# Moving every tile that the matrix engine reads onto a 128-byte line

## The chip, the cores and the metric

The kernel runs on one core of one Trainium2 chip. The metric is device time in microseconds (us). The kernel before took 677.31 us, the median of three runs (676.64 to 678.71).

## What is computed

The reference is windowed attention with sinks, followed by a two-layer feed-forward block. In short:

```python
scores = q @ k.T / sqrt(64)                 # 4 batches, 8 heads, 768 positions, head_dim 64
keep   = (key < 4) | ((0 <= row - key) & (row - key < 128))
a      = softmax(where(keep, scores, -1e9))
x      = (a @ v)                            # heads side by side: 3072 tokens x 512
h      = x @ w_in                           # 512 -> 2048
g      = max(h, 0) + alpha * min(h, 0)
out    = g @ w_out                          # 2048 -> 512
```

The weights arrive as 64-bit floats and the kernel turns each into a high and a low 32-bit part.

## The kernel before, in words

The 3072 tokens are handled as 12 chunks of 256 rows (`QC`), numbered `c`. The hidden dimension of 2048 is cut into 16 slices of 128, numbered `f`. A chunk has two parts of work. Its attention makes the rows `x`, held as a high part `xh` and a low part `xl`, each four blocks of 128 x 256. Then the feed-forward block runs over the 16 slices.

One step (c, f) of the feed-forward block has two groups of matmuls on the matrix engine (PE). The first group, `gemm1` on line L894, is 12 matmuls of 128x128 against 128x256: the stationary operand (loaded into the array ahead of the matmul) is a block of the weight tile `w`, and the moving operand (streamed through) is `xh` or `xl`. The scalar engine (ACT) and the vector engine (DVE) then make `g` (L898, L899) and split it into `gh` and `gl` (L900, L901). The second group, `gemm2`, is 6 matmuls of 128x128 against 128x512 (L931, L932, L929; the very last step has them on L916 to L918): here `gh` or `gl` is stationary and the weight tile `w` moves. `gemm2` of a step runs two steps (`LAG`) behind `gemm1`, so PE has other work while ACT and DVE make `g`.

Attention of the next chunk is spread over the steps of the current one. From chunk 2 on, a head's `q` and `k` are copied from the loaded tile `stage` into a tile `kq` (L561 to L565): `k` with a high part in 64 partitions and a low part in the other 64, and `q` as `qh` and `ql`. The scores are two matmuls per half head, L597 with `qh` stationary and L598 with `ql` stationary, and the moving operand is `k`, mostly 260 columns wide. In the tile before, `k` comes first (392 columns), then `qh`, then `ql`. The matmuls with the values are on L786 and L875. Heads alternate between two `kq` tiles. Chunks 0 and 1 read `stage` directly (L588).

A planner in the kernel (`Plan`) fixes the order of all instructions from estimated costs. Which of several buffers an operation gets also comes from it. It knows nothing of addresses. In the first microseconds PE runs fill matmuls (L1086) on a small tile `idle`, whose one column is read over and over, 512 columns wide.

Where a tile lies in SBUF follows from the order in which tiles are asked for and from their sizes, rounded up to 32 bytes. Each partition has the same layout, so one address stands for a tile. With the sizes in the code, the tiles that PE reads begin at these bytes past a multiple of 128 (from the addresses in the two built programs):

| tile | read by PE as | before | with the change |
|---|---|---|---|
| `xh`, `xl` | moving, gemm1 | 96 | 0 |
| `w` of slices 0 to 13 and 15 | stationary gemm1, moving gemm2 | 32 | 0 |
| `w` of slice 14 | the same | 64 | 0 |
| `gh`, `gl` | stationary, gemm2 | 96 | 0 |
| `k` in the two `kq` tiles, first half of the rows | moving, scores | 96 and 0 | 0 and 0 |
| the same, second half (132 columns on) | moving, scores | 112 and 16 | 16 and 16 |
| `qh`, `ql` in the two `kq` tiles | stationary, scores | 0 and 32 | 0 and 0 |
| `v` | stationary, values | 32 | 0 |
| `ident` | moving, transposes | 64 | 0 |
| `sinkT`, `vs` | sinks | 96 | 0 |
| `comb`, `wa` | moving, values | 0 | 0 |
| `stage`, `pt_` (read by PE in chunks 0 and 1 alone) | scores, transposes | 32, 64; 32, 64, 96 | 0, 32; 64, 96, 0 |

All blocks that a matmul takes out of these tiles begin a whole multiple of 128 bytes into the tile, except the second half of `k`.

Of the kernel before, what the change touches and what calls it, by code (L numbers as in the profile page):

```python
# [9 lines left out]
F32 = mybir.dt.float32  # L10
F32R = mybir.dt.float32r
# [4 lines left out]
I32 = mybir.dt.int32  # L16
# [3 lines left out]
P = 128  # L20
B, H, S, D = 4, 8, 768, 64
DM, DF = 512, 2048
NS = 4
WIN = 2 * P + NS
QC = 2 * P
KC = 3 * P + 2 * NS
CPB = S // QC
NCHUNK = B * CPB
NF = DF // P
# [49 lines left out]
class Plan:  # L79
# [20 lines left out]
    def held(self, tile_):  # L100
        v = Value(None)
        v.at = tile_
        return v

    def op(self, engine, cost, run, reads=(), writes=(), tail=0.09, mode=None, nbytes=0, other=None, locks=False):
        o = Op(engine, cost, tail, run, self.rank if engine == "PE" else None)
        o.ways = {engine: (cost, run)}
        if other:
            o.ways[other[0]] = other[1:]
        o.born = self.rank  # L110
        if engine == "PE":
            self.rank += 1
        o.mode, o.nbytes, o.index = mode, nbytes, len(self.ops)
        seen = []
        for group, writing in ((reads, False), (writes, True)):
            for x in group:
                v, key = x if isinstance(x, tuple) else (x, None)
                if v not in seen:
                    seen.append(v)
                keys = [k for k in set(v.wrote) | set(v.read) if key is None or k is None or k == key]  # L120
                for k in keys:
                    o.before.update(v.wrote.get(k, ()))
                    if writing:
                        o.before.update(v.read.get(k, ()))
                if writing:
                    for k in keys:
                        if key is None or k == key:
                            v.wrote.pop(k, None)
                            v.read.pop(k, None)
                    v.wrote.setdefault(key, []).append(o)  # L130
                else:
                    v.read.setdefault(key, []).append(o)
        for v in seen:
            v.left += 1
        o.values = seen
        o.takes = [v for v in seen if v.kind]
        o.locks = locks
        self.ops.append(o)
        return o
# [144 lines left out]
def dve(n, fast=False):  # L284
    return 0.07 + (0.52e-3 if fast else 1.04e-3) * n


def cast(n, psum=False):
    return (0.045 if psum else 0.092) + 0.84e-3 * n
# [32 lines left out]
def program(ctx, tc, qk, pairs, vp, vq, vs, w, par, out):  # L322
    nc = tc.nc
    const = ctx.enter_context(tc.tile_pool(name="const", bufs=1))
# [10 lines left out]
    def several(name, n, shape, dtype):  # L335
        plan.kind(name, [pool.tile(shape, dtype, name=f"{name}{i}") for i in range(n)])
# [2 lines left out]
    plan.kind("swap", [scratch.tile([4, P, P], F32, name=f"swap{i}") for i in range(2)])  # L339
    plan.kind("turns", [scratch.tile([4, P, 2 * 32], F32, name=f"turns{i}") for i in range(2)])  # L340
    trid = held(scratch.tile([P, 2, P], F32, name="trid"))
    several("stage", 2, [P, QC + KC], F32)
    several("kq", 2, [P, KC + 2 * QC], F32R)
    several("v", 4, [P, 3, 2, D], F32)
    several("pt_", 3, [P, 2, WIN], F32)
    several("comb", 5, [P, 4 * P], F32)
    several("wa", 2, [P, 2 * DM], I32)
    several("sink", 2, [P, 2, H, NS], F32)
    several("nm", 2, [P, H, 2], F32)
    several("sm", 2, [P, H, 2], F32)  # L350
    several("ri", 4, [P, 8], F32)
    several("jk", 3, [P, 2], F32)
    several("ts", 1, [P, 2, 4, 32], F32R)
    several("sinkT", 1, [P, QC], F32R)
    several("vs", 1, [P, DM], F32R)
    several("ob", 2, [P, DM], F32)
    several("xh", 2, [P, KT, QC], F32R)
    several("xl", 2, [P, KT, QC], F32R)
    several("g", 2, [P, QC], F32)
    several("gh", LAG + 1, [P, QC], F32R)  # L360
    several("gl", LAG + 1, [P, QC], F32R)

    size = const.tile([P, NF], F32, name="size")
    sizes = held(size)
    raws, fins = {}, {}

# [41 lines left out]
    stage, vtile, vst = {}, {}, {}  # L408
# [3 lines left out]
    def lend(f, shape, count):  # L412
        box = {}

        def part(i):
            if "tile" not in box:
                box["tile"] = const.tile([P, count, *shape], F32, tag=f"w{f}", name="lent")
            return box["tile"][:, i]
        out_ = []
        for i in range(count):  # L420
            v = held(None)
            v.bind, v.box = lambda i=i: part(i), box
            out_.append(v)
        lent[f] = out_
        return out_

    early = lend(NF - 1, [QC + KC], 3) + lend(NF - 2, [QC + KC], 1)
    shared = const.tile([P, 1, QC + KC + 4 * WIN], F32, tag=f"w{NF - 2}", name="lent")
    early[3].box["tile"] = shared[:, :, :QC + KC]
    early_v = lend(NF - 3, [3, 2, D], 4)  # L430

    def bound(v):
        if v.at is None:
            v.at = v.bind()
        return v.at

    def load_head(c, h):
# [4 lines left out]
        src = pairs[c, h // 2] if c in SPLIT else qk[c, h]  # L442
        op("SP", ISSUE, lambda: nc.sync.dma_start(bound(t), src), writes=[t], nbytes=4 * P * (QC + KC))

# [71 lines left out]
    masks = pool.tile([P, 3, WIN], BF16, name="masks")  # L516
    ident = const.tile([P, P], F32, name="ident")
    tri = pool.tile([P, 2, P], F32, name="tri")
    fm = const.tile([P, 2 * H], F32, name="fm")
    flag = const.tile([1, 1], I32, name="flag")  # L520

    setup("POOL", 0.2, lambda: nc.gpsimd.iota(rel[:, 0:P], pattern=[[-1, P]], base=P, channel_multiplier=1), (), ("rel",))
# [24 lines left out]
    xh, xl, prep, comb, sink, ptile_, sums, rinv, nms, wt = {}, {}, {}, {}, {}, {}, {}, {}, {}, {}  # L547
# [4 lines left out]
    def prep_head(c, h):  # L552
        st = stage.pop((c, h))
        if c in SPLIT:
            r = slice(h % 2 * D, (h % 2 + 1) * D)
            prep[c, h] = (st, r)
            return
        kq = val("kq")
        ks, qh, ql = [lambda s=s: kq.at[:, s] for s in (slice(0, KC), slice(KC, KC + QC), slice(KC + QC, KC + 2 * QC))]
        q_raw, k_raw = lambda: st.at[:, :QC], lambda: st.at[:, QC:]  # L560
        op("ACT", cast(KC), lambda: nc.scalar.copy(ks(), k_raw()), reads=[st], writes=[(kq, "k")])  # L561
        op("ACT", cast(QC), lambda: nc.scalar.copy(qh(), q_raw()), reads=[st], writes=[(kq, "q")])
        op("DVE", dve(KC), lambda: nc.vector.tensor_tensor(ks()[D:], k_raw()[D:], ks()[D:].bitcast(F32), ALU.subtract),  # L563
           reads=[st], writes=[(kq, "k")])
        op("DVE", dve(QC), lambda: nc.vector.tensor_tensor(ql(), q_raw(), qh().bitcast(F32), ALU.subtract),  # L565
           reads=[st, (kq, "q")], writes=[(kq, "l")])
        prep[c, h] = (kq, qh, ql, ks)

    def unit(c, h, u):
# [6 lines left out]
        qs = slice(u * P, (u + 1) * P)  # L576
        w0 = slice(0 if c % CPB or u else P, WIN)
        n = w0.stop - w0.start
# [24 lines left out]
    def soften(c, h, u, s):  # L603
        if u == 0:
            ptile_[c, h] = val("pt_")
        pt, nm, sm = ptile_[c, h], nms[c], sums[c]
        i = min((c % CPB) * 2 + u, 2)
        w0 = slice(0 if i else P, WIN)
# [9 lines left out]
    def finish_head(c, h):  # L618
# [5 lines left out]
        if c in SPLIT:  # L624
            op("POOL", 0.17, lambda: nc.gpsimd.tensor_copy(sk.at[:, :, h], pt.at[:, :, P:P + NS]), reads=[pt], writes=[(sk, h)])
            tp = bank(c, h, "pa")
            for u in range(2):
                o = 2 * u * P
                both = u > 0 or c % CPB > 0

# [5 lines left out]
            t = val("comb")  # L636
            o = P if c % CPB == 0 else 0
            op("ACT", cast(4 * P - o, True), lambda: nc.scalar.copy(t.at[:, o:], tp.at[:, o:]), reads=[tp], writes=[t],
# [10 lines left out]
        for u in range(2):  # L649
            if u == 0 and c % CPB == 0:  # L650
                op("DVE", 0.2, lambda: nc.vector.tensor_scalar(view()[:, 0], pt.at[:, 0, P + NS:], ri.at[:, 0:1], None, op0=ALU.mult),
# [13 lines left out]
    sinkT = {}  # L665
# [282 lines left out]
    def attention(c):  # L948
        def a_step(h, u):
            def run():  # L950
                if u == 0:
                    if h == 0 and c == PAIRED:
                        masks_in_order()
                    if h == 0 and c and c % CPB == 0:
                        vs_prep(c // CPB)
                    prep_head(c, h)
                    next_load()
                unit(c, h, u)
                if u == 1:
                    finish_head(c, h)  # L960
                    first = 1 if c >= PAIRED else 5
                    if h in range(first, first + (KT if c >= PAIRED else 2)):
                        load_v(c, h - first)
            return run
# [139 lines left out]
    with tc.If(bad != 0):  # L1104
# [3 lines left out]
        with tc.For_i(0, B, 1) as b:  # L1108
            for cc in range(CPB):
# [4 lines left out]
                for j in range(2):  # L1114
                    ob = gen.tile([P, DM], F32, tag="ob", name="ob", bufs=3)
# [162 lines left out]
```

## Time and profile before

| | |
|---|---|
| runs | 678.71, 677.31, 676.64 us, median 677.31 |
| profiled execution, first to last instruction | 676.2 us; its own device time is not shown, the span is 1.1 us under the median |
| busy share of the span | PE 98%, PE weight loads 86%, DVE 78%, ACT 59% |
| mean granted PE clock | 0.994 |
| gemm1 matmuls | 2304 |
| gemm2 matmuls on L931, L932, L929 | 382 each |

A PE row's busy time overlaps its neighbours', because a matmul starts before the one ahead of it has left the array. So the length of a matmul says little about its cost. What counts is the time from one start to the next, which is called spacing below. It is read from a timeline, where each row has a start to a hundredth of a microsecond; over a run of n matmuls the spacing is the distance of two starts divided by n.

### The profile page before, as it was taken

The numbers are of one execution on the slowest core, as the hardware profiler recorded it, in microseconds if no ns is written. First come the engines' busy times: TensorE is split into PE (matmuls) and PEld (weight loads), VectorE is DVE, ScalarE is ACT, GpSimd is POOL, SyncE is SP. The second block draws the span as 40 slices with busy tenths as digits, with TensorE's granted clock in tenths as the row PEclk, the third lists the DMA queues.
The fourth block names the chain that finished last, engine by engine and source line by source line (L and its number), as shares of the span: only waits on it lengthen the run. The fifth ranks groups of instructions, "written<-read, shape, count | busy, mean of one in ns | idle before, by whom it ended". The sixth has DMA issues, their size and how long they took to land.

```text
span 676.2 us, 13243 instructions
## 1 busy us (share of the span) xinstructions
PE 663.8 (98%) x4532; PEld 580.5 (86%) x4534; DVE 525.8 (78%) x1750; ACT 397.5 (59%) x1066; POOL 34.5 (5%) x115
## 2 busy tenths in 40 slices
PE   9989999999999999999999999999999999999996
PEld 4577898888989989989988988988998988998995
DVE  6999999968967976986986995995895994994331
ACT  6989888827636726736636735644744753853332
POOL 2110000001000000000000000010000000000000
PEclk9979999999999999999999999999999999999999
DMA  8684641424343453443443433552542543420001
GB/s 314 229 277 151 241 187 39 127 71 147 122 133 107 122 148 93 145 132 95 141 118 114 143 107 93 163 140 61 172 128 78 161 128 88 142 94 17 32 2 35
DMA packets 58683, 85.19 MB, mean 126 GB/s; under 512 B 9072, under 2 KB 35056, under 8 KB 58608
## 3 DMA queue, kind: packets, MB, share of 16 engines
q1 hardware_dynamic: 55056, 71.17, 34.7%
q10 hardware_dynamic: 3552, 13.11, 5.4%
q8 instruction: 37, 0.61, 0.4%
q14 instruction: 38, 0.31, 0.1%
HBM read 67.22 MB, written 17.04 MB: 125 GB/s over the span
## 4 chain that ended last, share of the span: by engine, by line
PE 83%; DVE 9%; ACT 5%; issue 2%; POOL 0%; DMA 0%; ACTq 0%; SPq 0%; POOLq 0%
PE bank L894 35%; PE bank L931 12%; PE bank L932 11%; PE bank L929 11%; PE bank L786 3%; PE bank L598 3%; PE bank L597 3%; PE bank L875 2%; DVE wa L396 2%; ACT pt L614 1%; ACT wa L382 1%; DVE wa L394 1%; DVE w L404 1%; DVE g L899 1%; DVE gl L901 1%
## 5 line engine op out<-in xcount | busy, mean ns | idle before, releaser
L894 PE MATMUL bank<-xh,w 128*128 128x256 f32 x1536 | 307.9, 283 | 0.4 <-DVE g L899 0.2
L894 PEld LDWEIGHTS bank<-xh,w 128*128 128x128 f32 x1536 | 250.6, 189 | 9.0 <-DVE g L899 3.0
L894 PE MATMUL bank<-xl,w 128*128 128x256 f32 x768 | 215.1, 280 | 0.1
L898 ACT ACTIVATE g<-bank,param 128x256 f32<-128x256 f32 x192 | 90.5, 472 | 117.4 <-PE bank L894 113.1
L931 PE MATMUL bank<-w,gh 128*128 128x512 f32 x382 | 151.7, 397 | 0.2 <-ACT gh L900 0.2
L932 PE MATMUL bank<-w,gh 128*128 128x512 f32 x382 | 150.1, 393 | 0.0
L894 PEld LDWEIGHTS bank<-xl,w 128*128 128x128 f32 x768 | 145.2, 189 | 4.4 <-DVE xl L808 0.3
L614 ACT ACTIVATE pt<-pt,nm 128x260 f32<-128x260 f32 (+1 forms) x192 | 94.5, 493 | 53.5 <-DVE nm L610 53.1
L899 DVE TENSOR_TENSOR g<-bank,g 128x256 f32<-128x256 f32 x192 | 79.7, 419 | 51.4 <-ACT g L898 50.9
L929 PE MATMUL bank<-w,gl 128*128 128x512 f32 x382 | 119.5, 394 | 0.0
L900 ACT CAST gh<-g 128x256 fp32r<-128x256 f32 x192 | 76.9, 404 | 59.7 <-DVE g L899 59.6
L901 DVE TENSOR_TENSOR gl<-g,gh 128x256 fp32r<-128x256 f32 x192 | 80.5, 423 | 26.5 <-ACT gh L900 23.0
L610 DVE CUSTOM_DVE_ANT_0 pt<-bank,masks 128x260 f32<-128x260 f32 (+1 forms) x192 | 75.0, 401 | 19.3 <-PE bank L598 15.5
L929 PEld LDWEIGHTS bank<-w,gl 128*128 128x128 f32 x382 | 70.7, 188 | 16.2 <-issue 0.7
L931 PEld LDWEIGHTS bank<-w,gh 128*128 128x128 f32 x382 | 71.9, 188 | 9.5 <-ACT gh L900 0.7
L932 PEld LDWEIGHTS bank<-w,gh 128*128 128x128 f32 x382 | 71.9, 188 | 8.3
L563 DVE TENSOR_TENSOR kq<-stage,kq 64x392 fp32r<-64x392 f32 x80 | 45.3, 566 | 2.7
L659 POOL TENSOR_TENSOR sink<-pt,ri 128x8 f32<-128x8 f32 x80 | 20.8, 264 | 504.7 <-DVE ri L644 358.8
L597 PE MATMUL bank<-kq 128*128 128x260 f32 (+1 forms) x160 | 44.4, 278 | 1.3 <-DVE nm L610 1.3
L598 PE MATMUL bank<-kq 128*128 128x260 f32 (+1 forms) x160 | 45.0, 281 | 0.0
L655 DVE CUSTOM_DVE_ANT_0 comb<-pt,ri 128x128 f32<-128x128 f32 x136 | 43.1, 343 | 0.4
L561 ACT CAST kq<-stage 128x392 fp32r<-128x392 f32 x80 | 40.9, 512 | 0.7 <-ACT pt L614 0.2
(130 smaller groups left out, 686.9 us busy)
## 6 DMA issues: line engine op xcount, KB each, us to landing
stage<-qk SPq DMA_DIRECT2D x80, 324.0 KB, 2.9
wraw<-w ACTq DMA_DIRECT2D x12, 1024.0 KB, 5.9
swap<-comb SPq DMA_DIRECT2D x36, 256.0 KB, 2.0
comb<-swap SPq DMA_DIRECT2D x36, 256.0 KB, 3.2
v<-vq SPq DMA_DIRECT2D x36, 192.0 KB, 2.5
out_dram<-ob SPq DMA_DIRECT2D x22, 256.0 KB, 3.5
wraw<-w SPq DMA_DIRECT2D x4, 1024.0 KB, 12.0
v<-vp SPq DMA_DIRECT2D x8, 192.0 KB, 6.9
```

The costliest lines, as they stand in the source:

```text
L597: nc.tensor.matmul(s[:, w0], qh()[:, qs], ks()[:, kw], start=True, stop=False)
L598: nc.tensor.matmul(s[:, w0], ql()[:, qs], ks()[:, kw], start=False, stop=True)
L610: op("DVE", dve(n), lambda: nc.vector.tensor_tensor_reduce(out=pt.at[:, u, w0], in0=s.at[:, w0], in1=masks[:, i, w0], scale=-0.125, scalar ...
L614: op("ACT", exp(n), lambda: nc.scalar.activation(pt.at[:, u, w0], pt.at[:, u, w0], AF.Exp, bias=nm.at[:, h, u:u + 1], scale=-1.0, accum_ou ...
L894: nc.tensor.matmul(h(), fin.at[:, 0, part, ks], rhs.at[:, kt], start=(kt == 0 and n == 0), stop=(kt == KT - 1 and n == 2))
L898: op("ACT", act(QC, True), lambda: nc.scalar.activation(g.at, h(), AF.Copy, scale=alt[:, f:f + 1]), reads=[bk, known("param")], writes=[g])
L899: op("DVE", dve(QC), lambda: nc.vector.tensor_tensor(g.at, h(), g.at, ALU.max), reads=[bk], writes=[g])
L900: op("ACT", cast(QC), lambda: nc.scalar.copy(gh.at, g.at), reads=[g], writes=[gh])
L901: op("DVE", dve(QC), lambda: nc.vector.tensor_tensor(gl.at, g.at, gh.at.bitcast(F32), ALU.subtract), reads=[g, gh], writes=[gl])
L929: nc.tensor.matmul(o2[j].at, gl.at[:, js], fin.at[:, 1, 0], start=False, stop=(f == NF - 1))
L931: nc.tensor.matmul(o2[j].at, gh.at[:, js], fin.at[:, 1, 0], start=(f == 0), stop=False)
L932: nc.tensor.matmul(o2[j].at, gh.at[:, js], fin.at[:, 1, 1], start=False, stop=False)
```

## The change

Two dummy widths are added to small tiles (`size`, `fm`) that lie ahead of the weights, so that the weight tiles begin on multiples of 128 bytes. The pools' tiles are asked for in another order: those that PE reads first, the tiles with odd sizes last. The tile `kq` is padded to a multiple of 32 floats, and inside it `qh` and `ql` now come first and `k` last. The instructions, their order on every engine, the buffers that they use and the semaphores that they wait for are the same in both built programs; only addresses differ.

```diff
@@ -24,6 +24,8 @@
 KC = 3 * P + 2 * NS
+LINE = 32
+KQ = -(-(KC + 2 * QC) // LINE) * LINE
@@ -339,28 +341,28 @@
     trid = held(scratch.tile([P, 2, P], F32, name="trid"))
-    several("stage", 2, [P, QC + KC], F32)
-    several("kq", 2, [P, KC + 2 * QC], F32R)
-    several("v", 4, [P, 3, 2, D], F32)
-    several("pt_", 3, [P, 2, WIN], F32)
-    several("comb", 5, [P, 4 * P], F32)
-    several("wa", 2, [P, 2 * DM], I32)
-    several("sink", 2, [P, 2, H, NS], F32)
-    several("nm", 2, [P, H, 2], F32)
-    several("sm", 2, [P, H, 2], F32)
-    several("ri", 4, [P, 8], F32)
-    several("jk", 3, [P, 2], F32)
-    several("ts", 1, [P, 2, 4, 32], F32R)
-    several("sinkT", 1, [P, QC], F32R)
-    several("vs", 1, [P, DM], F32R)
-    several("ob", 2, [P, DM], F32)
     several("xh", 2, [P, KT, QC], F32R)
     several("xl", 2, [P, KT, QC], F32R)
     several("g", 2, [P, QC], F32)
     several("gh", LAG + 1, [P, QC], F32R)
     several("gl", LAG + 1, [P, QC], F32R)
-
-    size = const.tile([P, NF], F32, name="size")
+    several("sinkT", 1, [P, QC], F32R)
+    several("vs", 1, [P, DM], F32R)
+    several("ob", 2, [P, DM], F32)
+    several("v", 4, [P, 3, 2, D], F32)
+    several("comb", 5, [P, 4 * P], F32)
+    several("wa", 2, [P, 2 * DM], I32)
+    several("ts", 1, [P, 2, 4, 32], F32R)
+    several("sink", 2, [P, 2, H, NS], F32)
+    several("kq", 2, [P, KQ], F32R)
+    several("stage", 2, [P, QC + KC], F32)
+    several("pt_", 3, [P, 2, WIN], F32)
+    several("nm", 2, [P, H, 2], F32)
+    several("sm", 2, [P, H, 2], F32)
+    several("ri", 4, [P, 8], F32)
+    several("jk", 3, [P, 2], F32)
+
+    size = const.tile([P, 2 * NF], F32, name="size")[:, :NF]
@@ -516,7 +518,7 @@
-    fm = const.tile([P, 2 * H], F32, name="fm")
+    fm = const.tile([P, 3 * H], F32, name="fm")[:, :2 * H]
@@ -556,7 +558,7 @@
         kq = val("kq")
-        ks, qh, ql = [lambda s=s: kq.at[:, s] for s in (slice(0, KC), slice(KC, KC + QC), slice(KC + QC, KC + 2 * QC))]
+        ks, qh, ql = [lambda s=s: kq.at[:, s] for s in (slice(2 * QC, 2 * QC + KC), slice(0, QC), slice(QC, 2 * QC))]
```

## The prediction

> **What bounds the kernel now.** I read the page first (busy shares and the chain that ended last), then the busy time in two windows, then the timeline of PE, because this change can only alter how fast PE streams.
>
> ```profile
> PE 663.8 (98%) x4532; PEld 580.5 (86%) x4534; DVE 525.8 (78%) x1750; ACT 397.5 (59%) x1066; POOL 34.5 (5%) x115
> PE 83%; DVE 9%; ACT 5%; issue 2%; POOL 0%; DMA 0%; ACTq 0%; SPq 0%; POOLq 0%
> 0.00:150.00 150.00, 144.45 (x928) 114.72 (x931) 135.76 (x355) 116.65 (x274) 12.36 (x40) 0.98 0.54 183
> 150.00:676.00 526.00, 519.40 (x3606) 465.78 (x3604) 390.03 (x1395) 280.85 (x793) 22.16 (x75) 1.00 0.37 110
> ```
>
> The first row is the page's busy time, the second its chain by engine, the last two are windows (columns: length, then PE, PE weight loads, DVE, ACT, POOL, granted clock, DMA share, GB/s). Up to 150 us DVE is busy for 135.76 of 150 us, since the weights are being converted. From 150 us on PE is busy for 519.40 of 526 us at clock 1.00, and DVE for only 390.03, 74%. PE sets the time there. So what is saved per matmul after 150 us shows in the time almost one for one, and what is saved before counts for little. The same windows for single lines count the matmuls in the second one:
>
> ```profile
> 150.00:676.00 526.00, 252.26 (x1908) 239.53 (x1908) 1.00 0.37 110
> 150.00:676.00 526.00, 125.97 (x319) 59.83 (x318) 1.00 0.37 110
> 150.00:676.00 526.00, 99.83 (x320) 59.87 (x320) 1.00 0.37 110
> ```
>
> These are L894 (1908 gemm1 matmuls, 159 steps of 12), L931 (319) and L929 (320). L932 follows each L931 one for one, so gemm2 has about 958.
>
> Now the spacing. In the last chunk no attention runs, so one step stands alone:
>
> ```profile
> 641.00 0.39 PE L931 MATMUL bank<-w,gh 128*128 128x512 f32 x1
> 641.91 0.62 PE L929 MATMUL bank<-w,gl 128*128 128x512 f32 x2
> 642.37 0.28 PE L894 MATMUL bank<-xh,w 128*128 128x256 f32 x1
> 643.19 0.28 PE L894 MATMUL bank<-xl,w 128*128 128x256 f32 x1
> 643.53 0.28 PE L894 MATMUL bank<-xl,w 128*128 128x256 f32 x1
> 643.76 0.39 PE L931 MATMUL bank<-w,gh 128*128 128x512 f32 x1
> ...
> 655.08 0.40 PE L931 MATMUL bank<-w,gh 128*128 128x512 f32 x1
> 656.48 0.28 PE L894 MATMUL bank<-xh,w 128*128 128x256 f32 x1
> 657.30 0.28 PE L894 MATMUL bank<-xl,w 128*128 128x256 f32 x1
> 657.65 0.28 PE L894 MATMUL bank<-xl,w 128*128 128x256 f32 x1
> 657.89 0.40 PE L931 MATMUL bank<-w,gh 128*128 128x512 f32 x1
> ```
>
> First step: six gemm2 matmuls take 642.37 - 641.00 = 1.37 us, 228 ns each; twelve of gemm1 take 1.39 us, 116 ns each; the step 2.76 us. Second step: 1.40 us (233 ns) and 1.41 us (117.5 ns), together 2.81 us. Within gemm1, three matmuls take 0.34 us in the first (643.19 to 643.53, 113 ns each) and 0.35 us in the second (117 ns each). So there are two paces, and the second is not caused by other engines' work: in the second step's last 0.8 us they do next to nothing.
>
> ```profile
> 657.10:657.90 0.80, 0.80 (x10) 0.80 (x9) 0.07 (x1) 0.00 (x0) 0.00 (x0) 1.00 0.00 0
> ```
>
> What would PE do if operands came at full pace? The nearest row is that of the fills, which read one column over and over:
>
> ```profile
> 7.52 1.25 PE L1086 MATMUL bank<-idle 128*128 128x512 bf16 x5
> ```
>
> Five start within 1.25 us less the last one's length. That length is that of a single fill:
>
> ```profile
> 19.63 0.38 PE L1086 MATMUL bank<-idle 128*128 128x512 bf16 x1
> ```
>
> So (1.25 - 0.38) / 4 = 218 ns for 512 columns, and half, 109 ns, for 256. Against that floor gemm2 loses 10 to 15 ns per matmul and gemm1 7 to 8.5 ns. The loss grows with the width, so it belongs mostly to streaming and not to changing weights. This loss is all that alignment can win.
>
> **The change part by part.** No instruction, wait or buffer is added, removed or moved, so no queue and no DMA costs anything new. Terms arise only from the spacing of PE's matmuls.
>
> *gemm2: `w` moves from 32 bytes past a line to 0.* The trace has one natural experiment: slice 14 has its `w` at 64, all others at 32. Its six matmuls in the last quiet stretch:
>
> ```profile
> 624.13 0.28 PE L894 MATMUL bank<-xl,w 128*128 128x256 f32 x1
> 624.36 0.40 PE L931 MATMUL bank<-w,gh 128*128 128x512 f32 x1
> 625.76 0.28 PE L894 MATMUL bank<-xh,w 128*128 128x256 f32 x1
> ```
>
> They take 1.40 us, 233 ns each, although the gemm1 ahead of them ran at the quick pace (two in 0.23 us up to 624.36, 115 ns). After a quick gemm1 the other slices take 228 ns. So the address does count: 32 bytes further from the line cost 5 ns. If the cost goes on falling towards the line, 32 to 0 wins another 5 ns: 958 x 5 ns = 4.8 us. Bounds: nothing, and the floor (12 ns in the middle, 11.5 us).
>
> *gemm1: `xh`, `xl` move from 96 to 0, `w` as stationary operand from 32 to 0.* No row shows this tile elsewhere. The floor would win 7 to 8.5 ns, nothing is the other bound. I take 4 ns, the distance between the two paces (113 and 117 ns) and about half of the loss: 1908 x 4 ns = 7.6 us. It is nearer to the middle than to an end, for the scores below speak against the floor.
>
> *Scores: `k` from 96 or 112 to 0 or 16.* Heads alternate between the two `kq` tiles, so both cases stand in the trace: first a head with `k` at 96, then one with `k` already on the line.
>
> ```profile
> 271.37 0.28 PE L597 MATMUL bank<-kq 128*128 128x260 f32 x1
> 271.61 0.28 PE L894 MATMUL bank<-xh,w 128*128 128x256 f32 x1
> ...
> 277.40 0.28 PE L597 MATMUL bank<-kq 128*128 128x260 f32 x1
> 277.64 0.29 PE L894 MATMUL bank<-xh,w 128*128 128x256 f32 x1
> ```
>
> Both pairs take 0.24 us, 120 ns per matmul, where the floor for 260 columns is 218 x 260 / 512 = 111 ns. Within the 10 ns that the timeline resolves for a pair, the line alone does not bring the floor. There are 160 pairs, so even 5 ns per pair is 0.8 us; I take 0.
>
> *Values and transposes* (L786, L875, `v` and `ident`): these are 32-bit matmuls that PE runs in several passes, more slowly than an operand can be read, and there are few; 0. *DVE and ACT* work on the same tiles at new addresses. No row tells what an address costs them; DVE has 526 - 390 = 136 us to spare after 150 us, and if its work there grew by 2%, 8 us, PE would still cover it: 0. Without that cover, before 150 us, 2% would cost 2.7 us. Before 150 us, DVE is the bound and I count 0 of the 396 gemm1 matmuls there.
>
> Sum: 4.8 + 7.6 = 12.4 us off the span of 676.2 us, 663.8 us; with the 1.1 us between span and median 664.9 us, so **665 us**.
>
> A page of the Trainium skill speaks against any effect: SBUF — State Buffer, in the box on SBUF "cachelines", gives lines of 16 bytes. Every start before is a multiple of 32 bytes, so each tile already lies on such a line and by that rule the time stays at 677.3 us. The slice at 64 bytes, 233 against 228 ns, does not fit it.
>
> **The rivals.**
>
> *No effect.* What PE loses would be a cost of reading 32-bit operands at this pace wherever they lie, and slice 14 would be slow for another reason (its tile lies apart from the others, ahead of them in SBUF). For: the two score pairs of equal length. Against: the slice. Time: 677.
>
> *The whole loss goes.* Both operands on the line, PE at the floor: a step is 12 x 109 + 6 x 218 = 2616 ns, against 2760 to 2810, so 144 to 194 ns in 159 steps, 23 to 31 us: 646 to 654. For: both paces exceed the floor with no other engine at work. Against: the score pair with `k` on the line; but there the stationary `ql` lay at 32, so the case of both on the line is not in the trace.
>
> *Slower: the two read streams of PE meet.* While a matmul streams, the next weights are loaded, and after the change both streams always begin on the same byte of a line. Before, they were 64 bytes apart (96 against 32) in both gemms; in gemm2 of slice 14 they were 32 apart (64 against 96) and it was 5 ns slower. Read this way the same row says that the change, at distance 0, costs 10 ns per gemm2 matmul against 64: 958 x 10 = 9.6 us, and gemm1 would hold the slow pace throughout, 117.5 against the middle 116.7, 1.5 us: 688. It costs from the point at which distance and not position counts; half of that, gemm2 alone at 233 ns and gemm1 at 117.5, gives 2.81 us a step against the middle of 2.785, 4 us: 681. Against: in the score pairs the streams were 96 bytes apart (96 against 0) and 32 apart (0 against 32) with no difference. The Trainium skill, TensorE: Matmul & The Clock Gate, section "Step-by-step: what each phase is for", holds that weights and moving operand have read ports of their own and do not take bandwidth from each other; no run here shows that by itself.
>
> *The change does not do what it says.* The second half of `k` still starts at 16 past a line, and `pt_` and `stage` are off it. They are few matmuls; the large groups all move, so this explains at most the scores.
>
> **How the numbers follow.** Partial gain (655 to 673 us) 0.45; the whole loss 0.14; no effect 0.21; slower 0.20. The predicted time is the likeliest case's, 665. A range for 8 in 10 takes in no effect and most of the whole gain and of the small slowdown: 648 to 681; the likeliest case alone has 655 to 673. A measurement of this kernel tells about 0.3%, 2 us, from no change. Faster by more than that: 0.45 + 0.14 and a little of "no effect" that comes out as 2 to 4 us, 0.61. Within: 0.19. Slower: 0.20.
>
> **What would show it.** Right: in the last chunk a step of 12 gemm1 and 6 gemm2 takes 2.68 to 2.72 us; gemm2 spacing 223 to 226 ns, slice 14 like all others; gemm1 near 112; DVE's and ACT's means unchanged; the window up to 150 us about as long. The whole loss: a step of 2.62 us, one pace only. No effect: 2.76 and 2.81 again, in whatever mix. Slower: gemm1 117 or more in every step and gemm2 at 233 or above. The prediction is wrong if the step keeps its two paces and only their mix changes, or if gemm1 and gemm2 go opposite ways.

## The result and the profile after

The changed kernel took 684.03 us (median of four runs, 683.60 to 684.59) beside 676.97 us for the kernel before: a ratio of 1.0095, with a 95% interval of 1.0079 to 1.0111. It is 7.1 us slower, where 665 was forecast. The profiled execution took 683.60 us with a span of 681.6 us. That is only 5.4 us more than the span of before, whose profile had the lower mean clock, 0.994 against 0.998; other runs of the kernel before at 0.992 to 0.994 have spans of 676.2 to 676.8 us, and at 0.998 of 674.4 to 675.1.

The page's busy time and its chain by engine, and the two windows that were shown of before (length, PE, weight loads, DVE, ACT, POOL, clock, DMA share, GB/s):

```profile
PE 669.3 (98%) x4532; PEld 585.8 (86%) x4534; DVE 526.0 (77%) x1750; ACT 399.7 (59%) x1066; POOL 35.0 (5%) x115
PE 89%; DVE 5%; ACT 4%; issue 1%; POOL 0%; ACTq 0%; POOLq 0%
0.00:150.00 150.00, 144.56 (x942) 114.61 (x944) 135.29 (x355) 117.33 (x275) 12.54 (x40) 1.00 0.53 184
150.00:676.00 526.00, 524.72 (x3596) 471.20 (x3592) 390.76 (x1395) 281.76 (x790) 22.43 (x75) 1.00 0.36 108
```

DVE and ACT have the same number of instructions as before; DVE is busy for 526.0 us against 525.8, ACT for 399.7 against 397.5. The chain that ended last runs even more through PE, 89% against 83%, and PE's spacing grew. One step of the last chunk, from PE's timeline of the changed kernel (start, length; gemm2 is now on L931, L933 and L934, gemm1 on L896):

```profile
637.53 0.40 PE L933 MATMUL bank<-w,gh 128*128 128x512 f32 x1
638.92 0.28 PE L896 MATMUL bank<-xh,w 128*128 128x256 f32 x1
639.75 0.28 PE L896 MATMUL bank<-xl,w 128*128 128x256 f32 x1
640.11 0.28 PE L896 MATMUL bank<-xl,w 128*128 128x256 f32 x1
640.35 0.40 PE L933 MATMUL bank<-w,gh 128*128 128x512 f32 x1
```

gemm2 takes 1.39 us (232 ns per matmul), where it took 1.37 or 1.40. gemm1 takes 1.43 us (119 ns), where it took 1.39 or 1.41; three of its matmuls take 0.36 us, 120 ns each, where it was 113 or 117. The step has gone from 2.76 or 2.81 us to 2.82. There is one pace left for gemm1, and it is slower than both paces before.

Over all matmuls after the first 150 us, with those that wait left out, the mean spacing went from 116.2 to 119.4 ns in gemm1 and from 231.3 to 231.8 ns in gemm2. With the prediction's counts that is 1908 x 3.2 + 958 x 0.5 = 6.6 us of the 7.1. The tables below give these two means for each run.

### The profile page after: what moved, and what is told of

Read it like the earlier page. It is cut to its first block, busy times and chain, and to the rows that moved or that the text cites. A ratio compares the mean times of both kernels' runs of the same rounds, so it can differ in the third digit from the quotient of the medians.

```text
span 681.6 us, 13243 instructions
## 1 busy us (share of the span) xinstructions
PE 669.3 (98%) x4532; PEld 585.8 (86%) x4534; DVE 526.0 (77%) x1750; ACT 399.7 (59%) x1066; POOL 35.0 (5%) x115
## 4 chain that ended last, share of the span: by engine, by line
PE 89%; DVE 5%; ACT 4%; issue 1%; POOL 0%; ACTq 0%; POOLq 0%
PE bank L896 39%; PE bank L933 13%; PE bank L934 12%; PE bank L931 12%; PE bank L788 3%; PE bank L600 3%; PE bank L599 3%; PE bank L877 2%; ACT pt L616 1%; PE bank L1088 1%; DVE wa L398 1%; ACT wa L384 1%; PE bank L861 1%; DVE pt L612 1%; DVE w L406 1%
## 5 line engine op out<-in xcount | busy, mean ns | idle before, releaser
L896 PE MATMUL bank<-xh,w 128*128 128x256 f32 x1536 | 313.6, 285 | 0.3
L896 PEld LDWEIGHTS bank<-xh,w 128*128 128x128 f32 x1536 | 252.5, 190 | 8.7 <-DVE g L901 2.6
L896 PE MATMUL bank<-xl,w 128*128 128x256 f32 x768 | 217.0, 283 | 0.1
L933 PE MATMUL bank<-w,gh 128*128 128x512 f32 x382 | 151.2, 396 | 0.0
L934 PE MATMUL bank<-w,gh 128*128 128x512 f32 x382 | 150.7, 395 | 0.0
L896 PEld LDWEIGHTS bank<-xl,w 128*128 128x128 f32 x768 | 146.0, 190 | 4.2 <-DVE xl L810 0.3
L931 PE MATMUL bank<-w,gl 128*128 128x512 f32 x382 | 119.4, 394 | 0.0
L931 PEld LDWEIGHTS bank<-w,gl 128*128 128x128 f32 x382 | 70.7, 188 | 16.1 <-issue 0.7
L933 PEld LDWEIGHTS bank<-w,gh 128*128 128x128 f32 x382 | 72.1, 189 | 9.3 <-ACT gh L902 0.8
L934 PEld LDWEIGHTS bank<-w,gh 128*128 128x128 f32 x382 | 72.2, 189 | 8.8
(130 smaller groups left out, 684.0 us busy)
```

The source lines that it names most:

```text
L896: nc.tensor.matmul(h(), fin.at[:, 0, part, ks], rhs.at[:, kt], start=(kt == 0 and n == 0), stop=(kt == KT - 1 and n == 2))
L931: nc.tensor.matmul(o2[j].at, gl.at[:, js], fin.at[:, 1, 0], start=False, stop=(f == NF - 1))
L933: nc.tensor.matmul(o2[j].at, gh.at[:, js], fin.at[:, 1, 0], start=(f == 0), stop=False)
L934: nc.tensor.matmul(o2[j].at, gh.at[:, js], fin.at[:, 1, 1], start=False, stop=False)
```

## The experiments

Three theories stood after the result. *Distance*: what counts is how far the moving operand starts from the stationary one that is loaded meanwhile. This is the prediction's third rival. *Position*: what counts is where an operand lies by itself. *Chance*: any new layout draws anew which pace the loop locks into. All kernels but one compute the whole result. But for the one with the swap alone, they differ from the changed kernel or the kernel before by tiles that only take up room:

```diff
+    pool.tile([P, n // 4], F32, name="pad_x")     # n bytes: xh, xl, g, and all behind them move
     several("xh", 2, [P, KT, QC], F32R)
...
+    pool.tile([P, n // 4], F32, name="pad_g")     # the same for gh, gl
     several("gh", LAG + 1, [P, QC], F32R)
...
+    pool.tile([P, n // 4], F32, name="pad_r")     # puts the rest back on a multiple of 128
     several("sinkT", 1, [P, QC], F32R)
```

**First set: shift the operands against each other by 64, 32 and 96 bytes, and all together by 32.** `e1_x64_g64` has pads of 64, 0 and 64 bytes, `e3_x32_g32` of 32, 0 and 96, `e4_x96_g96` of 96, 0 and 32. `e2_all32` widens the small tile ahead of the weights instead, so that all tiles behind it move together:

```diff
-    size = const.tile([P, 2 * NF], F32, name="size")[:, :NF]
+    size = const.tile([P, 2 * NF + 8], F32, name="size")[:, :NF]
```

> The changed kernel with xh, xl, gh and gl 64 bytes past a line; w, kq and all others stay on the line. Theory distance (what counts is how far, mod 128, the moving operand starts from the stationary one that is loaded meanwhile; 0 apart is slow, 64 apart is quick): gemm1 goes from 120 ns back to a mix of 113 and 118 ns, the time to 675 to 679 us. Theory position (what counts is where the moving operand alone lies; on the line is slow, off it is quick): gemm1's moving operand is off the line, so gemm1 gets quicker too, but gemm2's, w, stays on it; the time lands near 677 as well, so this run tells these two from the third only. Theory chance (any new layout draws anew which pace the loop locks into): anything from 675 to 686.

> The changed kernel with everything behind the first small tile 32 bytes further: moving and stationary operands all 32 past a line, 0 apart from each other as in the change. Distance: gemm1 stays at 120 ns, the time at 683 to 685 us. Position: no operand is on the line any more, gemm1 leaves 120 ns for 113 to 118, the time falls to 675 to 679. Chance: anything.

> The changed kernel with xh, xl, gh and gl 32 bytes past a line, w on it: moving 32 ahead of stationary in gemm1, 32 behind (96) in gemm2. Distance: between the two known cases, gemm1 at 114 to 119 ns, 677 to 682 us; if only 0 apart is bad, 677. Position: as in the run with 64, gemm1 113 to 118. Chance: anything.

> The changed kernel with xh, xl, gh and gl 96 bytes past a line, w on it: 96 apart in gemm1, 32 in gemm2. Distance: gemm2 may be 5 ns slower, as slice 14 was before at 32 apart, gemm1 114 to 119 ns; 678 to 684 us. Position: xh and xl lie where they lay before, so gemm1 is as before, 113 and 118 ns, and the time 675 to 679. Chance: anything.

| run | time, us | ratio to before (95%) | gemm1 ns | gemm2 ns |
|---|---|---|---|---|
| before | 677.2 | | 116.2 | 231.3 |
| change | 684.0 | 1.0095 (1.0079 to 1.0111) | 119.4 | 231.8 |
| all +32 | 683.9 | 1.0096 (1.0079 to 1.0113) | 119.4 | 231.8 |
| 64 | 680.6 | 1.0048 (1.0031 to 1.0065) | 117.1 | 232.9 |
| 32 | 680.6 | 1.0046 (1.0029 to 1.0062) | 117.1 | 232.9 |
| 96 | 684.9 | 1.0110 (1.0093 to 1.0127) | 119.3 | 232.9 |

The first row holds the median of before in the runs beside this set (676.97 us is the one beside the result), and each ratio is to the runs of before beside it. The run with 96 came out a little above the 678 to 684 us expected, the one with 64 above its 675 to 679.

The run with everything 32 bytes further decides between position and distance. No large operand lies on a line any more, and the time and both spacings are those of the change. A step of its last chunk, from its timeline:

```profile
641.10 0.40 PE L933 MATMUL bank<-w,gh 128*128 128x512 f32 x1
642.49 0.28 PE L896 MATMUL bank<-xh,w 128*128 128x256 f32 x1
643.92 0.40 PE L933 MATMUL bank<-w,gh 128*128 128x512 f32 x1
```

Again 1.39 and 1.43 us. Position falls, and so does chance as a rule for every new layout, since here a new layout gave the old means to a tenth of a nanosecond. But distance as I had put it is not right either: 64 apart gave 680.6 and not 677, although mod 128 it is the distance of the kernel before. Looked at mod 256, the two differ. Before, `xh` started 192 bytes past `w` and `w` 64 past `gh`; in the run with 64 it is the other way round, 64 and 192.

**Second set: distance mod 256, which gemm carries the loss, the swap alone, and PE alone.** `e7_x192_g192` has pads of 192, 0 and 64 bytes, `e9_x192_g256` of 192 and 64. `e8_kq_swap_alone` is the kernel before with one line of the change:

```diff
-        ... (slice(0, KC), slice(KC, KC + QC), slice(KC + QC, KC + 2 * QC))]
+        ... (slice(2 * QC, 2 * QC + KC), slice(0, QC), slice(QC, 2 * QC))]
```

The fourth is a program of its own. The moving and the stationary tile lie at the same place mod 256 and are read at shifted columns (4 bytes each):

```python
def pairs(n, m, s):                      # 24 equal matmuls of n columns
    for i in range(24):
        nc.tensor.matmul(banks[i % 2][:, :n], sta[:, s:s + P], mov[:, m:m + n], start=True, stop=True)
for n in (256, 512):
    for d in range(0, 128, 4):           # 0 to 496 bytes in steps of 16
        pairs(n, d, 0)
...                                      # both shifted; one of the two a repeated column; far shifts
```

> The changed kernel with xh, xl, gh and gl 192 bytes further: seen mod 128 the same as the run with 64, but mod 256 the moving operand of gemm1 is now 192 ahead of w, and w is 64 ahead of gh in gemm2, as in the kernel before. Theory distance mod 256: back to the kernel before, 676 to 678.5 us, gemm1 115 to 116.5 ns, gemm2 near 231. Theory distance mod 128: the same as the run with 64, 680 to 681.5 us, gemm1 117, gemm2 233. Chance: neither.

> The kernel before with the change's swap inside kq alone (q first, k behind, no padding), all addresses of tiles as before. Both distance theories: the scores are 320 of some 4500 matmuls, so at most 1 us either way: 676 to 678.5 us. If the swap carries the loss: 682 to 684.

> The changed kernel with xh and xl 192 bytes further but gh and gl 256 further, so gemm1 has the distance of the kernel before (192) and gemm2 that of the change (0). Distance mod 256: gemm1 at 115 to 116.5 ns, gemm2 at 231.5 to 232, time 677 to 679 us: gemm1 carries nearly all of the loss. If gemm2 carries it: 682 to 684.

> No attention and no feed-forward block: PE alone runs 24 equal matmuls at a time on tiles whose start is shifted in steps of 16 bytes, 256 and 512 columns, and writes zeros out. Distance: with the stationary operand fixed the spacing runs through a pattern with the distance of the two starts (period 128 or 256 bytes), 113 to 120 ns for 256 columns and 224 to 234 for 512, and it stays when both are shifted together; with one operand a single repeated column the spacing falls to 109 and 216 to 218 whatever the place of the other. Position: the moving operand alone, with repeated weights, still shows the pattern. A cost of streaming wherever it lies: moving alone keeps 113 ns or more at every place.

The program for PE alone first. These rows of its timeline each hold a run of equal matmuls (start, length of the run, count); the spacing is the length less the last matmul's own 0.28 us (0.39 us at 512 columns), divided by the count less one. They are, in this order: 256 columns at distance 0, at 112 and at 192; 512 columns at 0 and at 192; the moving operand with one repeated weight column (L42), 256 and 512 columns; the weights with one repeated moving column (L46), 256 and 512 columns.

```profile
12.57 2.08 PE L38 MATMUL bank<-mov,sta 128*128 128x256 f32 x16
32.38 2.09 PE L38 MATMUL bank<-mov,sta 128*128 128x256 f32 x17
46.48 2.09 PE L38 MATMUL bank<-mov,sta 128*128 128x256 f32 x17
106.80 3.56 PE L38 MATMUL bank<-mov,sta 128*128 128x512 f32 x15
172.71 4.60 PE L38 MATMUL bank<-mov,sta 128*128 128x512 f32 x19
358.82 2.09 PE L42 MATMUL bank<-mov,sta 128*128 128x256 f32 x17
380.68 4.52 PE L42 MATMUL bank<-mov,sta 128*128 128x512 f32 x19
422.08 2.07 PE L46 MATMUL bank<-mov,sta 128*128 128x256 f32 x17
435.68 4.32 PE L46 MATMUL bank<-mov,sta 128*128 128x512 f32 x19
```

So 120 ns at distance 0 and 113 at 112 and 192; 226 at 0 and 234 at 192 for 512 columns; 113 and 229 for moving alone; 112 and 218 for weights alone. All sixteen distances, from the starts of the 5th to the 21st matmul of each group, which the trace has to a nanosecond:

| distance, bytes | 0 | 16 | 32 | 48 | 64 | 80 | 96 | 112 |
|---|---|---|---|---|---|---|---|---|
| 256 columns, ns | 119.9 | 118.6 | 116.6 | 118.4 | 117.8 | 120.0 | 120.1 | 113.3 |
| 512 columns, ns | 226.9 | 231.6 | 233.5 | 233.3 | 228.9 | 230.9 | 233.9 | 231.5 |

| distance, bytes | 128 | 144 | 160 | 176 | 192 | 208 | 224 | 240 |
|---|---|---|---|---|---|---|---|---|
| 256 columns, ns | 118.6 | 118.7 | 117.2 | 119.4 | 113.4 | 119.2 | 118.3 | 117.1 |
| 512 columns, ns | 232.1 | 233.3 | 233.9 | 233.1 | 233.3 | 234.6 | 233.3 | 226.7 |

From 256 to 496 bytes the same sixteen numbers come again, within 0.2 ns but for the first pair (1.0 ns at 512 columns). With both operands shifted by 32 or by 128 bytes, distances 0, 64 and 128 give 119.6, 117.8 and 118.6 at 256 columns, nearly as without the shift. Further distances of 512 to 4096 bytes, and these plus 192, again give 119.6 and 113.4. So the spacing goes by the distance mod 256, but not by it alone: at distance 192, with both operands shifted by 128 bytes (first row) and by 32 (second row), the matmuls ran at (2.40 - 0.28) / 18 = 118 ns and not at 113.

```profile
294.77 2.40 PE L38 MATMUL bank<-mov,sta 128*128 128x256 f32 x19
306.14 2.40 PE L38 MATMUL bank<-mov,sta 128*128 128x256 f32 x19
```

Both groups came right behind one at distance 128. The seven groups at distance 192 that settled at 113.3 or 113.4 came behind one at 176 or 0. So this distance has two paces for 256 columns, and either holds to the end of its group. In PE alone the place and the group ahead changed together, so it does not tell which of them decides. Distances other than 0, 64, 128 and 192 were all run behind one neighbour only, and may have a second pace too.

A pace is not there from the first matmul either. At 512 columns and distance 0, behind a group at 192, the first six spacings are 225, 236, 229, 232, 231 and 227 ns (first row, 230 in the mean), and the later ones are 226.7 (second row):

```profile
500.16 1.77 PE L38 MATMUL bank<-mov,sta 128*128 128x512 f32 x7
501.76 3.79 PE L38 MATMUL bank<-mov,sta 128*128 128x512 f32 x16
```

With that said, the lowest spacings of a narrow moving operand are at 112 and 192, those of a wide one at 240, 0 and 64: one of the worst distances for gemm1 is nearly the best for gemm2.

The prediction took its floor from the fills, 109 and 218 ns. Weights alone come near it at all four places tried. Moving alone does not: 113 to 117 and 229 to 232 ns at seven places. No distance tried gave less than 113.3 and 226.7, so half or more of the loss that I had hoped to win (7 to 8.5 ns in gemm1, 10 to 15 in gemm2) was there at every distance. What streaming costs while no weights are read was not measured, since repeated weights are still read; nor was a bf16 operand that is streamed, and the fills are bf16.

Two pages of the Trainium skill were weighed in the prediction. TensorE: Matmul & The Clock Gate ("Step-by-step: what each phase is for") has weights and moving operand on read ports of their own that do not take from each other. Here 256 columns cost 113 to 117 ns with a repeated weight column and 113 to 120 with a stream of weights, by their distance, so where the weights lie does change the time of the moving operand. SBUF — State Buffer (the box on SBUF "cachelines") has lines of 16 bytes; the pattern has a period of 256 and changes at steps of 16 within it.

Now the kernels, with the spacing that PE alone has at their distances:

| run | gemm1 distance | PE alone | measured | gemm2 distance | PE alone | measured | time, us |
|---|---|---|---|---|---|---|---|
| before | 192 | 113.4 or 117.8 | 116.2 | 64 | 228.9 | 231.3 | 677.2 |
| change | 0 | 119.9 | 119.4 | 0 | 226.9 | 231.8 | 684.0 |
| 64 | 64 | 117.8 | 117.1 | 192 | 233.3 | 232.9 | 680.6 |
| 32 | 32 | 116.6 | 117.1 | 224 | 233.3 | 232.9 | 680.6 |
| 96 | 96 | 120.1 | 119.3 | 160 | 233.9 | 232.9 | 684.9 |
| 192 (`e7`) | 192 | 113.4 or 117.8 | 115.7 | 64 | 228.9 | 230.6 | 676.3 |
| 192 and 256 (`e9`) | 192 | 113.4 or 117.8 | 116.1 | 0 | 226.9 | 228.8 | 675.5 |

The run with 192 has the layout of the change but for three tiles, lies the same as the run with 64 mod 128, and is back at 676.3 us (ratio 0.9982, 0.9973 to 0.9992), where that one took 680.6. Its timeline, gemm1 (L898) and then gemm2 up to the next piece of work:

```profile
640.68 0.28 PE L898 MATMUL bank<-xh,w 128*128 128x256 f32 x1
641.50 0.28 PE L898 MATMUL bank<-xl,w 128*128 128x256 f32 x1
641.84 0.28 PE L898 MATMUL bank<-xl,w 128*128 128x256 f32 x1
642.06 0.39 PE L935 MATMUL bank<-w,gh 128*128 128x512 f32 x1
643.44 0.27 PE L1052 MATMUL bank<-ident,worst 128*1 128x128 f32 x1
```

gemm1 takes 1.38 us (115 ns), three of its matmuls 0.34 us as in the kernel before, gemm2 1.38. With gemm2 left at the change's distance (`e9`) the time is 675.5 us (ratio 0.9968, 0.9957 to 0.9978): gemm1's distance carries the loss. Values, transposes and scores have the change's distances in this run and in `e7`, so they carry none of it. A step of `e9`:

```profile
638.33 0.39 PE L935 MATMUL bank<-w,gh 128*128 128x512 f32 x1
639.69 0.28 PE L898 MATMUL bank<-xh,w 128*128 128x256 f32 x1
641.10 0.39 PE L935 MATMUL bank<-w,gh 128*128 128x512 f32 x1
```

gemm2 takes 1.36 us and gemm1 1.41, the slower pace of distance 192. The expectation of 677 to 679 was too high, for it had gemm2 at 231.5 to 232, and it came to 228.8. Of the distances, only gemm1's differs between this run and the change, yet gemm2 gained 3 ns. In most steps of the change's last chunk gemm2 runs 233, 236, 229, 232, 231, 227 ns: but for the first, these are the spacings with which PE alone began at distance 0 when it came from another, and six matmuls end before the settled pace. In most steps of `e9` there, all six run at 226 or 227. The swap alone took 678.2 us (ratio 1.0006, 0.9996 to 1.0016): no difference that can be told.

**Third set: the other half, and the best layout by the pattern.** `e10_g192_alone` has 192 bytes ahead of `gh` and 64 behind `gl`. `e12_before_gh64` is the kernel before with one pad of 64 bytes ahead of `gh`. `e11_best_by_map` is `e9` with slice 14's `w` on the same place mod 256 as the others, by this line:

```diff
-    fm = const.tile([P, 3 * H], F32, name="fm")[:, :2 * H]
+    fm = const.tile([P, 3 * H + 32], F32, name="fm")[:, :2 * H]
```

> The changed kernel with gh and gl alone 192 bytes further: gemm2 has the distance of the kernel before (w 64 ahead of gh), gemm1 that of the change (0). By the spacings measured for PE alone (256 columns: 120.0 at 0 against 113.3 at 192; 512 columns: 226.9 at 0 against 228.9 at 64): gemm1 stays at 119.4, gemm2 at 230 to 232, time 682.5 to 685 us; gemm1 carries the loss. If gemm2 carries it: 677.

> The changed kernel with xh and xl 192 bytes further, gh and gl 256 further, and slice 14's w moved by 128 so that it lies like the others mod 256. By the map of PE alone both gemms are at their best distance (192 and 0) in all 16 slices: gemm1 115.5 to 116.2, gemm2 228 to 229, slice 14 like the rest; 674 to 675.5 us, 0.3 to 0.5% under the kernel before. If distances mod 256 were not the cause: no different from 675.5 or back above 677.

> The kernel before with one 64-byte tile ahead of gh, nothing else: gemm2's distance goes from 64 to 0, gemm1's stays 192. By the map gemm2 gains 2 ns on 958 matmuls: 674.5 to 676 us. If the line of 128 bytes were what counts: gh at 32 and w at 32 both still off it, 677.

| run | distances | gemm1 ns | gemm2 ns | time, us | ratio (95%) |
|---|---|---|---|---|---|
| `e10` | 0 and 64 | 119.1 | 230.7 | 682.1 | 1.0080 (1.0062 to 1.0098) |
| `e11` | 192 and 0, all slices | 116.3 | 228.3 | 674.9 | 0.9964 (0.9951 to 0.9977) |
| `e12` | 192 and 0, not slice 14 | 116.6 | 229.2 | 676.7 | 0.9993 (0.9985 to 1.0002) |

`e10` leaves gemm1 at distance 0 and keeps 5.1 of the 7.1 us; 682.5 to 685 was expected. Its step:

```profile
638.79 0.40 PE L935 MATMUL bank<-w,gh 128*128 128x512 f32 x1
640.17 0.28 PE L898 MATMUL bank<-xh,w 128*128 128x256 f32 x1
641.61 0.40 PE L935 MATMUL bank<-w,gh 128*128 128x512 f32 x1
```

gemm2 1.38 us, gemm1 1.44. `e11` is faster than both kernels, 0.36% under the kernel before, as expected. Its step takes 638.52 to 641.30, 2.78 us, gemm2 1.36 of it and gemm1 1.42, again the slower pace of distance 192:

```profile
638.52 0.39 PE L935 MATMUL bank<-w,gh 128*128 128x512 f32 x1
639.88 0.28 PE L898 MATMUL bank<-xh,w 128*128 128x256 f32 x1
641.30 0.39 PE L935 MATMUL bank<-w,gh 128*128 128x512 f32 x1
```

Putting slice 14 in line cannot be told in the time: 674.9 against 675.5 for `e9`, with intervals that overlap; but slice 14's gemm2 went from 233 ns in `e9` to between 227 and 229 in chunks 3 to 10. `e12` is a miss: 674.5 to 676 was expected and 676.7 measured, not to be told from the kernel before. Its gemm2 gained 2.1 ns as forecast, 2.0 us over 958 matmuls, but gemm1, which nobody touched, lost 0.4 ns, 0.8 us, and the rest of the gain is not found in these two means. gemm1 held the slower pace of its distance more often: 61% of its spacings after 150 us, waits left out, lie at 117 to 119 ns, against 49% in the kernel before. So here a new distance in gemm2 changed the pace of gemm1. A step of `e12` (gemm2 is on L932, gemm1 on L895), 1.36 and 1.41 us:

```profile
638.79 0.39 PE L932 MATMUL bank<-w,gh 128*128 128x512 f32 x1
640.15 0.28 PE L895 MATMUL bank<-xh,w 128*128 128x256 f32 x1
641.56 0.39 PE L932 MATMUL bank<-w,gh 128*128 128x512 f32 x1
```

## Why the prediction was wrong

- **What bounds the kernel** was right: DVE's busy time stayed, ACT's grew by 2.2 us away from the longest chain, and 6.6 of 7.1 us are accounted for by gemm1 and gemm2 after the first 150 us.
- **The term of gemm1 failed, and by its sign.** It had -4 ns on 1908 matmuls; the change gave +3.2 ns. The step took the distance between the two paces for something that a line would win. What counts is the distance of two starts mod 256, and the kernel before had gemm1 at 192, where PE alone runs at 113.4 or 117.8 ns; the change put it at 0, one of the three worst of sixteen.
- **The term of gemm2 failed in its reading of slice 14.** It had -5 ns on 958 matmuls; the change gave +0.5 ns. The row was right, 233 against 228 ns, and does show that addresses count. I read it as 32 bytes further from a line. It was 224 instead of 64 bytes between `w` and `gh`, for which PE alone gives 233.3 and 228.9 ns. In the changed kernel slice 14 lies on the line and is still the odd one, with its distance at 128: its gemm2 runs from 629.07 to 630.47, 1.40 us against 1.39 in the step shown above.

```profile
629.07 0.39 PE L933 MATMUL bank<-w,gh 128*128 128x512 f32 x1
630.47 0.28 PE L896 MATMUL bank<-xh,w 128*128 128x256 f32 x1
```

- **The floor** of 109 and 218 ns was no floor for these matmuls. So the rival in which the whole loss goes could not come about, and half of a loss was not there to be won.
- **The slower rival** had the mechanism, the two read streams, and the right side. Its sizes were wrong in both parts: gemm2 at distance 0 cost 0.5 ns and not 5 to 10, and gemm1, which it had at 117.5, went to 119.4. Its 681 to 688 us hold the measured time by errors that cancel. I gave it 0.20, and set it back for the score pairs, read as 96 and 32 bytes apart. That reading was wrong: `k` and `q` lie in one tile, so their distance is the same in both `kq` tiles (96 - 0 and 0 - 32 are both 96 mod 128), and the pairs compared a distance with itself.
- **No effect** and the 16-byte lines fell with the change itself, and the part on the swap (0 counted) held: 678.2 us with it alone.
- **The range** ended at 681, where that rival began.

The two paces of gemm1 in the kernel before, 113 and 118 ns, are the two that PE alone has at distance 192, so no other engine is needed for them. In the last chunk the quick one holds step after step up to one small matmul, and the slow one for the next six steps:

```profile
645.14 0.27 PE L1048 MATMUL bank<-ident,worst 128*1 128x128 f32 x1
```

`xh` and these slices' `w` lie at the same places mod 256 on both sides of it, so there the place does not decide. That what PE ran just ahead does is argued from this row and from PE alone, and no run tests it by itself. What in the chip holds a pace, and why the pattern of distances is what it is, stays open.

## What to carry to other kernels

Where PE streams 32-bit operands without a pause, look at the distance mod 256 bytes between the moving tile and the stationary tile that is loaded during it, and not at lines. In PE alone 256 columns were quickest at 112 and 192, 512 columns at 240, 0 and 64, and the worst distance cost 6% of the narrow matmul and 3.5% of the wide one. Measure the kernel after it: a distance can have two paces, and one group of matmuls can change the pace of the next. A tuned kernel may owe its time to a layout that nobody chose, so shift one tile against the other before aligning all of them to the same boundary. An odd row in a trace, like slice 14 here, has several differences from its neighbours; list them all (place, distance, mod which power of two) before one is taken for the cause.

## What the runs showed that was not expected

Shifting every tile by 32 bytes reproduced 683.9 us and both spacings to 0.1 ns, so, as far as this one shift shows, the time hangs on differences of addresses and not on the addresses. For PE alone the cost of a 128x256 matmul ran from 113.3 to 120.1 ns and that of a 128x512 one from 226.7 to 234.6 over sixteen distances, with a period of 256 bytes and no other engine at work. At one distance, 192, the narrow matmul ran at 113.4 or at 117.8 ns, each for a whole group. A moving operand that is streamed costs at least 113 and 229 ns even against a repeated weight column, where one repeated moving column against streamed weights costs 112 and 218 to 219.
